# Moving spreads, value casts and one output evacuation between engines and batches in a fused attention and feed-forward kernel

## The chip, the cores and the metric

The kernel runs on 1 core of one Trainium2 chip. The metric is device time in microseconds (us), lower is better. Most executions of this kernel agree within about 1 %. Below, TensorE, VectorE, ScalarE and GpSimd are the engines that the profile calls PE, DVE, ACT and POOL, and SyncE (SP) issues transfers.

## The reference

```python
# attention: 8 batches, 8 heads, 576 positions, head size 64
scores = (q @ k.T) / 8                       # per batch and head
# heads 0-3: the last 32 positions; heads 4-7: every 4th of the last 128
attn = softmax(where(mask, scores, -1e9))
x = (attn @ v), heads side by side           # 4608 tokens x 512
# feed-forward
h = x @ w_in                                 # 512 -> 2048
g = h * sigmoid(beta * h)
out = g @ w_out                              # 2048 -> 512, float32
```

## The kernel before

The tokens go through the feed-forward part in nine tiles of 512. While TensorE does tile t, the steps of the attention of batch t+1 are slipped in between its matmul groups, in an order written down by hand:

```python
SECOND = "K2 Q2 K3 Q3 v0 S20 v1 S21 S22 S23 ... V10 X00 V11 X01 X10 X11".split()   # beside tile 0
THIRD  = "d0 d1 v0 S20 S21 S22 k0 S23 v1 V20 S30 k1 V21 S31 q0 ...".split()        # beside tile 1
# S: scores and exp (from the third batch on, a mask multiplied in on GpSimd)
# V: values times scores, then 1/sum on VectorE;  X: transpose back to xT
# d, k, q: spreads (VectorE copies transposed data into zero-padded tiles)
# v0, v1: casts of the dilated heads' values, v2 / v4, v5: of the plain heads'
```

The third batch's q and k come by a detour: a casting write to a scratch in DRAM (GpSimd's queue), then four transposing loads on SyncE's queue, and behind these the loads of its values:

```python
for kind in "kq": cast_qk(2, kind)        # GpSimd: scratch write
for kind in "kq": load_dil(2, kind)       # SyncE: kdT, qdT
for kind in "kq": load_plain(2, kind)     # SyncE: kpT, qpT
...
at("X20", load_vd, b + 1, SQ)             # SyncE: values, behind the four transposes
```

A step's instructions go into each engine's queue in the order of the list, and every queue is worked off in order. One feed-forward group is 4 matmuls of 128x512; "o" groups (output part) have w_out in place of w_in:

```python
tnh = tanh(beta/2 * hps)                  # ScalarE
g   = (tnh + 1) * hps                     # VectorE, frees the PSUM bank
...
nc.scalar.mul(out=osb, in_=ops, mul=0.5)  # an output group leaves PSUM
```

The softmax here doesn't subtract the row's maximum and nothing guards it: scores larger than these inputs give would overflow.

Of the kernel before, what the change touches and what calls it, by code (L numbers as in the profile page):

```python
# [11 lines left out]
ALU = mybir.AluOpType  # L12
# [5 lines left out]
STEPS = (  # L18
    "S20 S21 S22 k0 S23 k1 V20 S30 q0 V21 S31 q1 V22 S32 q2 V23 S33 q3 V30 X20 S00 V31 S01 X21 V32 "
    "S02 V33 S10 V00 X30 S11 V01 S12 X31 V10 X00 V11 X01 X10 X11"  # L20
).split()
# [4 lines left out]
    "z1 z2"  # L26
).split()
SECOND = (
    "K2 Q2 K3 Q3 v0 S20 v1 S21 S22 S23 K0 K1 S30 V20 S31 Q0 V21 S32 V22 S33 V23 V30 S00 "
    "V31 X20 v2 S01 V32 S02 V33 S10 X21 S11 V00 X30 S12 V01 X31 V10 X00 V11 X01 X10 X11"  # L30
).split()
THIRD = (
    "d0 d1 v0 S20 S21 S22 k0 S23 v1 V20 S30 k1 V21 S31 q0 V22 S32 q1 V23 S33 q2 q3 V30 X20 S00 V31 "
    "S01 X21 V32 S02 V33 v2 S10 V00 X30 S11 V01 S12 X31 V10 X00 V11 X01 X10 X11"
).split()


@with_exitstack
def kernel(
# [10 lines left out]
    nc = tc.nc  # L50
# [43 lines left out]
    def bank(dt=FP32):  # L94
# [32 lines left out]
    k1 = [xT[:, 2 * i:2 * i + 2, 2 * S:2 * S + WIN + S] for i in range(2)]  # L127
    q1 = [qq[i][:].rearrange("p a b c d -> p (a b c d)").rearrange(
        "p (x h t) -> p x h t", x=2, h=2) for i in range(2)]
# [14 lines left out]
    def zeros_kz():  # L144
        for i in range(2):
            nc.gpsimd.memset(kz[i][64:128, :, :, 0], 0.0)
            nc.gpsimd.memset(kz[i][0:64, :, :, 1], 0.0)
# [51 lines left out]
    def build_masks_d():  # L199
        for hf, lo in enumerate(LO):  # L200
            band(mask_d[hf][:].rearrange("p a b n -> p (a b) n"), DQ[hf], -lo, WIN - 1 - lo,
                 1.0, 0.0)
# [26 lines left out]
    def load_w_in(c0, c1):  # L229
        nc.gpsimd.dma_start(  # L230
            out=w_in_bf[:, :, c0:c1], in_=moe_w_in[:, c0:c1].rearrange("(c p) d -> p c d", p=P))

    def load_w_out(g):
        nc.gpsimd.dma_start(
            out=w_out_bf[:, g * 4:(g + 1) * 4, :],
            in_=moe_w_out[g * 4 * P:(g + 1) * 4 * P, :].rearrange("(c p) d -> p c d", p=P))
# [86 lines left out]
    def cast_v(b, n, eng):  # L323
        if n == 2 or n > 3:
            h = slice(0, 4) if n == 2 else slice(2 * n - 8, 2 * n - 6)
            copy_on(eng)(out=vp[b % 2][:, h, :, 0:D], in_=vp_st[b % 2][:, h])
        else:
            f, K = (slice(n, n + 1), DK[n]) if n < 2 else (slice(0, 2), 96)
            copy_on(eng)(  # L329
                out=vd[b % 2][0:K, f].rearrange("p f h T e -> p (f h T) e")[:, :, 0:D],  # L330
                in_=vd_st[0:K, f].rearrange("p f h T d -> p (f h T) d"))
# [147 lines left out]
    def attention_step(b, name):  # L479
        if name[0] == "W":  # L480
            for n in range(int(name[1:])):
                nc.tensor.matmul(warm_ps[:], lhsT=warm_w[:, 0:P], rhs=warm_w[:], start=True, stop=True)
        elif name[0] == "H":
            early[0] = -1
            slot_h(0, int(name[1:]), (2, 3))
        elif name[0] in STEP:
            STEP[name[0]](b, *[int(c) for c in name[1:]])
        else:
            eng = (nc.scalar if name[0] == "v" and (b, name) in ((1, "v2"), (2, "v0"), (2, "v1"), (2, "v2")) else
                   nc.gpsimd if b == 0 and name in ("v1", "v4", "v5") else nc.vector)  # L490
            BRING[name[0]](b, int(name[1:]), eng)

# [37 lines left out]
    def slot_o(t, tb, part):  # L530
        if (t, tb) == (NTT - 1, 3):
            last_o(t, tb, part)
            return
        if part == 0:
            if t > NTT - 3 and tb:
                o_t[t, tb] = psum_at.tile([P, HD], FP32, name="at")
            elif t == 0 and tb == 2:
                o_t[t, tb] = psum_h.tile([P, HD], FP32, name="h_ps")
            else:
                o_t[t, tb] = psum_o.tile([P, HD], FP32, name="o_ps")  # L540
        ops = o_t[t, tb]
        for fb in range(4 * part, 4 * part + 4):
            nc.tensor.matmul(  # L543
                ops[:], lhsT=g_t[t, fb][:, tb * P:(tb + 1) * P], rhs=w_out_bf[:, fb, :],
                start=(fb == 0), stop=(fb == NFB - 1))
        if part == 3:
            osb = osb_pool.tile([P, HD], FP32, name="osb")
            nc.scalar.mul(out=osb[:], in_=ops[:], mul=0.5)  # L548
            later.append([2, lambda: store(t * NTOK + tb * P, osb)])


# [27 lines left out]


    def steps(b):
        return SECOND if b == 1 else THIRD if b == 2 else STEPS

    def extras(b):
        e = {}
        at = lambda name, fn, *a: e.setdefault(steps(b).index(name), []).append(lambda: fn(*a))
        V, A, G = nc.vector, nc.scalar, nc.gpsimd
        SQ = nc.sync
        if b + 1 < B:
            if b > 1:  # L590
                if b == 2:
                    at("S20", gate, raw[2, "q"][0:1, 0:1])
                for kind in "kq":
                    at("S20", cast_qk, b + 1, kind)
                at("X20", load_vd, b + 1, SQ)
                at("X20", load_vp, b + 1, SQ)
            if b == 1:
                at("X20", load_vd, b + 1, SQ)
                at("X20", load_vp, b + 1, SQ)
            if b > 1:  # L600
                for kind in "kq":
                    at("V21", load_dil, b + 1, kind)
                for kind in "kq":
                    at("V30", load_plain, b + 1, kind)
            if b > 1:
                at("S11", spread_dil, b + 1, 0, V)
                at("V01", spread_dil, b + 1, 1, V)
                at("X00", cast_v, b + 1, 3, G)
                at("X01", cast_v, b + 1, 2, G)
        return e  # L610


    SQ, G, A, V = nc.sync, nc.gpsimd, nc.scalar, nc.vector
# [20 lines left out]
    for name in FIRST:  # L634
        if name == "v1":
            attention_step(0, "v1")
            build_neg_p()
            for c0, c1 in ((0, 256), (256, 512), (512, 1024)):
                load_w_in(c0, c1)
            continue  # L640
        if name == "v5":
            for n in "kq":
                load_tok(1, n, 1)
            load_w_in(1024, 2048)
            make_identity(nc, ident_f[:])
        if name == "X10":
            build_beta()
        attention_step(0, name)
# [12 lines left out]
    for kind in "kq":  # L661
        load_plain(2, kind)
    load_w_out(3)
    zeros_kz()
    build_masks_d()
    build_masks_p()

# [1 line left out]
    at_once = [3, 2] + [1] * (NTT - 3) + [4]  # L669
    WORK = {"S": 3, "V": 3, "X": 2, "d": 3, "K": 3, "Q": 3, "k": 0, "q": 0, "v": 1}  # L670
    left = []
    first = lambda n: max(0, (n - 4) // 2) if n < 14 else 3 * n - 37
    for t in range(NTT):
        slots = []
        n = len(left)
        for fb in range(NFB):
            slots.append((slot_h, t, fb, (0, 1)) if (t, fb) in h_t else (slot_h, t, fb))
            while left and n - len(left) < n * (fb + 1) // NFB:
                slots.append(left.pop(0))
        left = [(slot_o, t, tb, part) for tb in range(4) for part in range(4)]  # L680
        if t == 0:

            left = [(slot_o, 0, tb, part) for part in range(4) for tb in range(3)] + left[12:]
            for n, tb in ((10, 0), (13, 1)):
                left.remove((slot_o, 0, tb, 0))
                slots.insert(n, (slot_o, 0, tb, 0))
        now = 4 * at_once[t] - (2 if t == 0 else 0)
        slots += left[:now]
        left = left[now:]
        b = t + 1  # L690
        work = list(enumerate(steps(b))) if b < B else []
        e = extras(b) if b < B else {}
        e0 = list(work)
        room = [(1 if fn is slot_h else 2) if n >= FROM.get(t, 0) else 0
                for n, (fn, *_) in enumerate(slots[:-2])]
        total, whole, done, seen = sum(room), sum(WORK[s[0]] for m, s in work), 0, 0
        for n, (fn, *args) in enumerate(slots):
            fn(*args)
            seen += room[n] if n < len(room) else 0
            while work and (done * total < whole * seen if t else len(e0) - len(work) < first(n)):  # L700
                m, name = work.pop(0)
                done += WORK[name[0]]
                for x in e.get(m, []):
                    x()
                attention_step(b, name)
            tick()
# [32 lines left out]
```

## Time and profile before

| | before |
|---|---|
| time, median of 3 runs | 335.06 us (334.36 to 336.41) |
| profiled execution | span 332.5 us |
| tile 0, tile 1, tile 2, each later full tile | 42.95, 34.44, 31.21, 33.09 us |

A tile is counted here from the weight load of its first matmul group to that of the next tile. In the page's list of busy time, TensorE leads by far (busy us, share of span, instructions):

```profile
PE 315.6 (95%) x2426; PEld 167.0 (50%) x2426; DVE 194.9 (59%) x432; ACT 199.0 (60%) x382; POOL 131.8 (40%) x172
```

The 5 % that TensorE is idle lie in the first 125 us and in the last slice, where the kernel runs out.

### The profile page before, as it was taken

The page shows a single profiled execution, that of the slowest core. Times are in us where ns is not written, and L with a number is a line of the kernel's source. Part 1 is how long each engine was busy: PE and PEld are TensorE (multiplying, and loading weights), DVE is VectorE, ACT ScalarE, POOL GpSimd, SP SyncE. Part 2 cuts the span into 40 slices and gives each one's busy share as a digit, 9 for nine tenths or more (in the row PEclk, how much of TensorE's full clock was granted, in tenths as well). Part 3 has the DMA queues.
Part 4 walks back from the last instruction along what each step waited for, and adds up shares of the span by engine and source line. Part 5 has one row for each costly group of instructions (what it writes and reads, how often), then busy time and mean ns, then how long its engine had stood idle before and what let it go on. Part 6 is the DMA issues. An engine that isn't in the chain of part 4 may idle for free.

```text
span 332.5 us, 6380 instructions
## 1 busy us (share of the span) xinstructions
PE 315.6 (95%) x2426; PEld 167.0 (50%) x2426; DVE 194.9 (59%) x432; ACT 199.0 (60%) x382; POOL 131.8 (40%) x172
## 2 busy tenths in 40 slices
PE   8888989997899899999999999999999999999995
PEld 3653456544455455555555555555555544444444
DVE  4668585479657775777376737673766344344400
ACT  3577566685757666666666666666666545355511
POOL 8883595133385346533653365335533000000000
PEclk9999999999999999999999999999999999999999
DMA  6999999999899795999598958792011210011131
GB/s 113 205 199 196 216 255 172 202 199 197 170 163 157 139 190 111 147 208 146 103 176 170 149 103 175 176 142 63 3 34 32 63 35 33 32 34 32 32 95 65
DMA packets 64927, 42.63 MB, mean 128 GB/s; under 512 B 48896, under 2 KB 58784, under 8 KB 64512
## 3 DMA queue, kind: packets, MB, share of 16 engines
q1 hardware_dynamic: 57264, 25.58, 41.2%
q0 software_dynamic: 7632, 16.64, 27.7%
q8 instruction: 19, 0.31, 0.4%
q14 instruction: 12, 0.10, 0.1%
HBM read 39.32 MB, written 16.52 MB: 168 GB/s over the span
## 4 chain that ended last, share of the span: by engine, by line
PE 80%; DMA 6%; DVE 5%; ACT 3%; POOL 3%; issue 1%; POOLq 0%; ACTq 0%; DVEq 0%
PE h_ps L505 30%; PE o_ps L543 28%; PE at L543 5%; DMA w_out_bf<-in_moe_w_out_dram 4%; PE at L443 4%; PE at L460 3%; DVE g L515 2%; DMA xT<-in_k_dram 2%; PE at L410 2%; PE at L417 2%; PE at L505 2%; ACT tnh L512 1%; PE at L358 1%; PE h_ps L543 1%; DVE qq L294 1%
## 5 line engine op out<-in xcount | busy, mean ns | idle before, releaser
L515 DVE SCALAR_TENSOR_TENSOR g<-tnh,h_ps 128x512 bf16<-128x512 bf16 x130 | 88.8, 684 | 90.0 <-ACT tnh L512 89.4
L505 PE MATMUL h_ps<-xT,w_in_bf 128*128 128x512 bf16 x520 | 131.0, 379 | 2.6 <-DVE g L515 2.1
L512 ACT ACTIVATE tnh<-h_ps,beta_half 128x512 bf16<-128x512 f32 x130 | 89.4, 687 | 57.6 <-PE h_ps L505 53.7
L543 PE MATMUL o_ps<-w_out_bf,g 128*128 128x512 bf16 x464 | 116.9, 379 | 0.7 <-DMA w_out_bf<-in_moe_w_out_dram 0.7
L505 PEld LDWEIGHTS <-w_in_bf 128*128 128x128 bf16 x576 | 51.5, 98 | 52.9 <-issue 3.4
L543 PEld LDWEIGHTS <-g 128*128 128x128 bf16 x560 | 50.2, 97 | 48.7 <-issue 1.0
L425 POOL TENSOR_TENSOR pt<-pt,mask_d 96x384 bf16<-96x384 bf16 (+1 forms) x48 | 36.8, 776 | 50.6 <-ACT pt L423 50.0
L423 ACT ACTIVATE pt<-at 128x384 bf16<-128x384 f32 (+2 forms) x107 | 45.9, 439 | 16.6 <-PE at L410 8.6
L450 DVE TENSOR_TENSOR xs<-at,rcp 48x256 bf16<-48x256 f32 (+2 forms) x91 | 42.1, 463 | 8.9 <-PE at L460 4.8
L425 POOL TENSOR_TENSOR pt<-pt,mask_PP 128x384 bf16<-128x384 bf16 x24 | 22.8, 950 | 37.5 <-ACT pt L423 37.4
L443 PEld LDWEIGHTS <-pt 128*128 128x128 bf16 (+2 forms) x448 | 24.3, 97 | 14.9 <-DVE vd L329 1.2
L548 ACT ACTIVATE osb<-o_ps 128x512 f32<-128x512 f32 x29 | 17.3, 597 | 19.4 <-PE o_ps L543 19.4
L417 PEld LDWEIGHTS <-kdT 128*96 128x96 bf16 (+1 forms) x128 | 14.3, 120 | 10.9 <-issue 1.5
L446 DVE RECIPROCAL rcp<-at 48x4 f32<-48x4 f32 (+2 forms) x91 | 16.0, 176 | 6.0 <-PE at L443 5.3
L543 PE MATMUL at<-w_out_bf,g 128*128 128x512 bf16 x80 | 19.4, 379 | 0.0
L460 PE MATMUL at<-ident_b,xs 96*128 96x96 bf16 (+1 forms) x224 | 17.9, 199 | 1.5 <-DVE xs L450 1.0
L460 PEld LDWEIGHTS <-xs 96*128 96x128 bf16 (+1 forms) x224 | 13.2, 96 | 11.1 <-issue 1.8
L443 PE MATMUL at<-vd,pt 96*128 96x65 bf16 (+1 forms) x244 | 17.3, 193 | 0.7 <-DVE vd L329 0.7
L417 PE MATMUL at<-qzd,kdT 128*80 128x96 bf16 (+1 forms) x122 | 17.1, 226 | 0.8 <-DVE qzd L282 0.8
L425 POOL TENSOR_TENSOR pt<-pt,mask_FP 128x384 bf16<-128x384 bf16 x12 | 10.9, 911 | 16.1 <-ACT pt L423 16.1
L505 PE MATMUL at<-xT,w_in_bf 128*128 128x512 bf16 x56 | 13.8, 379 | 1.4 <-DMA w_in_bf<-in_moe_w_in_dram 1.4
L474 ACT COPY xT<-at 128x384 bf16<-128x384 bf16 (+1 forms) x32 | 12.7, 396 | 2.6 <-PE at L460 2.6
(115 smaller groups left out, 255.1 us busy)
## 6 DMA issues: line engine op xcount, KB each, us to landing
vp_st<-in_v_dram SPq DMA_DIRECT2D x12, 384.0 KB, 8.9
qk<-in_k_dram POOLq DMA_DIRECT2D x6, 576.0 KB, 7.0
qk<-in_q_dram POOLq DMA_DIRECT2D x6, 576.0 KB, 10.4
vd_st<-in_v_dram SPq DMA_DIRECT2D x6, 384.0 KB, 5.3
w_out_bf<-in_moe_w_out_dram POOLq DMA_DIRECT2D x4, 512.0 KB, 17.6
vd_st<-in_v_dram SPq DMA_DIRECT2D x6, 320.0 KB, 6.2
out_dram<-osb SPq DMA_DIRECT2D x7, 256.0 KB, 3.5
out_dram<-osb SPq DMA_DIRECT2D x8, 224.0 KB, 2.4
```

The lines of the kernel that those rows point to most:

```text
L417: nc.tensor.matmul(sc[0:K, a, 0:2 * n], lhsT=kd[b][:, rp, h4, DO[hf]:DO[hf] + K], rhs=qzd[b % 2][:, :, rp, h4, hf * DQ[0]:hf * DQ[0] + n], ...
L423: nc.scalar.activation(out=w, in_=sc[0:K, :, 0:2 * n], func=ACT.Exp, scale=SCALE)
L425: nc.gpsimd.tensor_tensor(out=w, in0=w, in1=mask[0:K], op=ALU.mult)
L443: nc.tensor.matmul(pv[:, a, h2, :], lhsT=pt[x][0:K, c:c + P], rhs=rhs, start=True, stop=True)
L446: nc.vector.reciprocal(out=rcp[0:n, 0:m], in_=pv[0:n, :, :, D])
L450: nc.vector.tensor_tensor(out=xs_t[b, x, jx][:, a0:a0 + m], in0=pv[0:n, :, :, 0:D], in1=rcp[0:n, 0:m].unsqueeze(3).to_broadcast([n, m, 2, ...
L460: nc.tensor.transpose(xp[:, a * n:(a + 1) * n], xs[:, a].rearrange("p h d -> p (h d)"), ident_b[0:n, 0:n])
L505: nc.tensor.matmul(hps, lhsT=w_in_bf[:, kt, fb * P:(fb + 1) * P], rhs=xT[:, kt, t * NTOK:(t + 1) * NTOK], start=(kt == 2), stop=(kt == 1))
L512: nc.scalar.activation(out=tnh[:], in_=hps, func=ACT.Tanh, scale=beta_half[:, fb:fb + 1])
L515: nc.vector.scalar_tensor_tensor(out=g[:], in0=tnh[:], scalar=1.0, in1=hps, op0=ALU.add, op1=ALU.mult)
L543: nc.tensor.matmul(ops[:], lhsT=g_t[t, fb][:, tb * P:(tb + 1) * P], rhs=w_out_bf[:, fb, :], start=(fb == 0), stop=(fb == NFB - 1))
L548: nc.scalar.mul(out=osb[:], in_=ops[:], mul=0.5)
```

## The change

Its intent is to take work off VectorE and ScalarE where they hold up TensorE, in tiles 0 and 1, and to bring forward the weights that arrive late. Its core:

```diff
-SECOND: "K2 Q2 K3 Q3 v0 S20 v1 S21 ..."            -> no v0, v1, v2
+SECOND: "K2 Q2 K3 Q3 S20 S21 ..."
-THIRD:  "d0 d1 v0 S20 S21 S22 k0 S23 v1 V20 S30 k1 V21 S31 q0 V22 S32 q1 V23 S33 q2 q3 V30 ..."
+THIRD:  "S20 S21 S22 q0 S23 V20 S30 q1 V21 S31 q2 V22 S32 q3 V23 S33 V30 ..."
+FOURTH: as the later batches, with q3 ahead of S33, V31 ahead of S00 and X21 ahead of S01
 # third batch's spreads, during the second batch's attention, on VectorE
+                at("V10", spread_dil, b + 1, 0, V)
+                at("V11", spread_dil, b + 1, 1, V)
+                at("X01", spread_k, b + 1, 0, V)
+                at("X10", spread_k, b + 1, 1, V)
 # third batch's dilated value casts: from ScalarE to GpSimd, ahead of its masks
+                if b == 2:
+                    at("S20", cast_v, b, 0, G)
+                    at("S20", cast_v, b, 1, G)
 # second batch's value casts: from VectorE and ScalarE to GpSimd
     load_w_out(3)
+    for n in range(2):
+        cast_v(1, n, G)
     zeros_kz()
+    for n in (4, 5):
+        cast_v(1, n, G)
 # weights: first half of this piece of w_in ahead of the second batch's q and k
+            load_w_in(1024, 1536)
             for n in "kq":
                 load_tok(1, n, 1)
-            load_w_in(1024, 2048)
+            load_w_in(1536, 2048)
 # two output groups of tile 0 one h group later
-            for n, tb in ((10, 0), (13, 1)):
+            for n, tb in ((11, 0), (14, 1)):
 # one evacuation of tile 0
-            nc.scalar.mul(out=osb[:], in_=ops[:], mul=0.5)
+            if t == 0 and tb == 1:
+                nc.vector.tensor_single_scalar(out=osb[:], in_=ops[:], scalar=0.5, op=ALU.mult)
+            else:
+                nc.scalar.mul(out=osb[:], in_=ops[:], mul=0.5)
```

(The pacing of the second batch's steps is also refitted to the shorter list.)

## The prediction

> **What bounds the kernel now.** I read first the page's slices, then the busy time by stage (cut where a token tile of the second part begins), then TensorE in order of time. The slices say where there is anything to win:
>
> ```profile
> PE   8888989997899899999999999999999999999995
> PEclk9999999999999999999999999999999999999999
> ```
>
> TensorE is at full clock throughout, and the digits below 9 lie before about 125 us. Behind that it never waits: the tiles from 130.7 us on take 33.09 us each with 33.07 busy. So the end is set by TensorE, and a microsecond that it stops waiting before 130 us is a microsecond off the end. By stage (the h matmuls of tile 0 begin in full at 24.72, of tile 1 at 64.72, tile 2 at 99.33, tile 3 at 130.70; columns: window, wall, then busy us and instruction counts of PE, PEld, DVE, ACT, POOL, clock, DMA share, GB/s):
>
> ```profile
> 24.72:64.72 40.00, 36.00 (x358) 20.22 (x357) 26.83 (x55) 25.61 (x51) 20.90 (x32) 1.00 1.14 210
> 64.72:99.33 34.61, 30.61 (x240) 15.86 (x238) 23.60 (x50) 23.80 (x46) 15.83 (x18) 1.00 0.99 176
> 99.33:130.70 31.37, 30.05 (x238) 16.12 (x237) 22.13 (x48) 20.57 (x41) 15.74 (x18) 1.00 0.93 152
> 130.70:163.79 33.09, 33.07 (x254) 17.69 (x252) 21.48 (x48) 21.48 (x42) 16.11 (x18) 1.00 0.89 156
> ```
>
> TensorE idles 4.0 us in tile 0, 4.0 in tile 1, 1.3 in tile 2: 9.3 us is all that there is. The timeline of TensorE names the waits (in brackets: idle before, releaser):
>
> ```profile
> 33.22 1.04 PE L505 MATMUL at<-xT,w_in_bf 128*128 128x512 bf16 x4 [1.36 <-DMA w_in_bf<-in_moe_w_in_dram]
> ...
> 36.33 1.02 PE L543 MATMUL o_ps<-w_out_bf,g 128*128 128x512 bf16 x4 [0.70 <-DMA w_out_bf<-in_moe_w_out_dram]
> ...
> 45.75 0.62 PE L358 MATMUL at<-ident_b,xT 64*64 64x64 bf16 x18 [1.15 <-DVE g L515]
> ...
> 69.97 0.50 PE L417 MATMUL at<-qzd,kdT 128*96 128x192 bf16 x4 [0.76 <-DVE qzd L282]
> ...
> 78.57 1.02 PE L505 MATMUL h_ps<-xT,w_in_bf 128*128 128x512 bf16 x4 [1.08 <-DVE g L515]
> ...
> 80.46 1.02 PE L505 MATMUL h_ps<-xT,w_in_bf 128*128 128x512 bf16 x4 [0.74 <-DVE g L515]
> ...
> 113.28 0.34 PE L410 MATMUL at<-qq,kz 128*128 128x96 bf16 x4 [1.30 <-DVE qq L294]
> ```
>
> Each is a target of the change: the first two are weights that arrive late, the rest are VectorE late with a spread, or with the product g because spreads and casts stand in its queue.
>
> **What the Trainium skill says.** "GPSIMD Engine Reference", section Engine selection, has two-input work about twice as slow on GpSimd as on VectorE, and one-input work "roughly line-rate". The trace agrees on the casts: GpSimd's 96x2048 cast took 1.89 us, so I take 0.95 to 1.0 us for half of it; ScalarE's 96x1024 took 1.03. "SBUF — State Buffer", section SBUF: two separate sides, calls the port pair that VectorE and GpSimd share an exclusive lock. The trace fits: VectorE's value casts at 43 to 47 us, while GpSimd cleared kz, took 1.87 and 1.35 us, against 0.62 at best for this cast. "Trainium Kernel Development and Optimization", section Key Constraints, says that transfers issued from SyncE and GpSimd run on the same 16 DMA engines and interleave. The trace agrees: the third batch's value loads, issued in the busiest stretch, took 7.7 and 8.5 us, where the medians of the like are 5.3 and 6.2.
>
> **The change part by part.**
>
> Tile 0 (second batch's attention). The w_in load is halved and its first half goes ahead of a q/k load, so the 1.36 us wait should go. The first w_out block still lands at 22.03 + 14.25 = 36.3 us, but the order of instructions shows that one h group (4 x 0.216 = 0.86 us) and one transposing step (12 transposes, 0.40) now run before TensorE needs it. Work that used to follow 36.33 is done by then: 1.26 us won, not 2.06, with a smaller wait left. The value casts leave VectorE (1.87 + 1.35 us beside g), and the transposes behind 45.75 no longer wait for a g; I count 0.9 of that 1.15. At the end two output groups instead of one lie behind the last normalizations, and cover the two dilated spreads (0.45 us each) put between them. Their data is just there: that transpose is issued at 54.5 and lands 5.1 us later, at 59.6. Sum: tile 1 starts some 2.3 us early, near 62.4.
>
> On GpSimd the moved casts wait for values that land at 43.2 and 44.5 us (issued at 25.7 and 27.6, 17.5 and 16.9 us under way), then kz (6 us), two half casts (0.82 each) and the masks (8.2) follow to about 61.5. Before, masks ended at 54.6 and GpSimd waited 7.6 us until 62.2 for the gate. This fits into that wait and costs nothing.
>
> Tile 1 (third batch). VectorE loses two dilated spreads (0.92 us in all) and two k spreads (0.61 + 1.03), ScalarE two value casts (1.03 each). But **the third batch's value casts now stand in GpSimd's queue ahead of the masks of its attention**, and their data is late:
>
> ```profile
> 60.19 1.03 SPq L320 DMA_DIRECT2D vd_st<-in_v_dram  x2
> ...
> vd_st<-in_v_dram SPq DMA_DIRECT2D x1, 384.0 KB, 7.7
> vd_st<-in_v_dram SPq DMA_DIRECT2D x1, 320.0 KB, 8.5
> ```
>
> These loads queue on SyncE behind four transposes, which wait for the second q/k scratch write (37.93 + 16.6 = 54.5 us). TensorE being earlier moves none of this. So values land at 60.2 + 7.7 = 67.9 and 60.7 + 8.5 = 69.2. Before, ScalarE took the first at 68.97, and the second not until 73.86; GpSimd's masks did not depend on them. Now: second cast from 69.2 to 70.2, mask of the first score group to 71.1, of the second to 72.1 (0.91 each). The first value product V20 reads 32 columns past its own group, so its last weight load waits for the second mask too (the order shows both waits): it ends near 72.15. TensorE would be there after 6 groups (5.2 us), four score groups (0.5) and small waits, at 62.4 + 6 = 68.4. **A new wait of about 3.7 us**; tile 0's gain and more is spent in it.
>
> What it buys: V20 now stands two h groups earlier in TensorE's order, so its time is not to be compared with 73.07 directly. From V20 to the last part of tile 0's outputs the kernel before took 73.07 to 89.09, 16.02 us, with VectorE busy for 13.91: VectorE's stretch. The same stretch has now 11 h groups instead of 9. TensorE: 13 groups of 0.864 = 11.2, 7 score groups 1.1, 7 value groups of 0.14 = 1.0, two transposes 0.37, in all 13.7. VectorE: 11 g of 0.68 = 7.5, normalizations 3.7, three q spreads 1.5, in all 12.7; the k spreads (1.64) and one q spread are gone. So TensorE leads, plus 0.4 of small waits: 14.1. That output part starts at 72.15 + 14.1 = 86.3, 2.8 us before 89.09. The 10.24 us from there to tile 2 stay.
>
> Tile 2 (fourth batch). Its last q spread moves ahead of one g in VectorE's order (0.67 us) and a value group and an h group stand before the score group that waits for it. Of the 1.30 I count 1.0. One vector osb (some 0.6 us) for one on ScalarE is hidden. Tiles 3 to 7 have the same order as before.
>
> **Sum:** 335.06 - 2.8 - 1.0 = 331.3 us.
>
> **Rivals.**
> (a) The waits simply go. Of the waits named above, 1.26 + 0.9 in tile 0, 0.76 + 1.08 + 0.74 and two of 0.3 in tile 1, 1.0 in tile 2 make 6.3, so 328.8. For it: no engine is full in tile 1. Against it: the values' landing time above, which no part of the change moves. If they landed 2 us earlier, as in later batches, this is the result.
> (b) GpSimd becomes the bound further on. For it: casts, masks and the shared lock. Against it: it was busy 15.8 of 34.6 us in tile 1, and after V20 its masks need 0.9 us to about 2 us of TensorE. If slow casts (1.4 us each, as one of 80x1024 took 1.47) and one more stall come, 332.5 to 333.
> (c) VectorE stalls in front of the moved spreads, as qdT lands at 59.6. Tile 1 then starts up to 1 us later, but V20 has 3.7 us of slack against that: no difference.
>
> **Range and chances.** The landing of the values carries most of the error: a microsecond there is a microsecond. The tile 1 stretch is good for 0.7 either way, tile 2 for 0.4. I say 331.3, 329.3 to 333.4. Over 2% faster means below 328.4: only rival (a) with nothing lost, 0.07. Slower by 2% would need over 6.7 us of new waits beyond the one I know: 0.01.
>
> **What would show it.** The w_in wait at 33 us gone and the w_out wait shorter; tile 1 starting at 62 to 63; then TensorE idle for 3 to 4 us at 68 to 72, released by a GpSimd mask, with GpSimd waiting for the vd_st transfer until 68 to 69; no idle over 0.8 us from VectorE at 75 to 90; tile 2 starting near 96.5, tile 3 near 127; from there 33.1 us a tile. I am wrong if V20 runs by 69 or 70, if tile 1 starts later than 65, or if the idle of VectorE's making stays.

## The result

The changed kernel took 331.23 us in the median of 4 runs, 330.29 to 335.36, against 334.93 us before (4 runs). A ratio here is the mean time of one kernel's runs over that of the other's of the same rounds, so not quite the ratio of the medians: 0.9874, 95 % interval 0.9837 to 0.9911. Executions over 1.5% slower than the fastest of the same kernel are left out of the means. The same, unchanged file ran twice more among the experiments: 1.0003 (0.9939 to 1.0066) and 0.9946 (0.9898 to 0.9993). All three are within 2 % of before.

The first profile fell in a slow execution (335.36 us), the second (after_again) had a stretch of half clock. The third (after_third, span 329.5 us) ran at full clock from start to end, as the profile of before did, and started its tile 0 at the same moment (21.65 and 21.72 us). These two are compared. By stage, columns as in the prediction:

```profile
24.65:63.46 38.81, 35.21 (x351) 20.18 (x356) 25.75 (x57) 23.92 (x49) 22.75 (x33) 1.00 1.20 206
63.46:97.22 33.76, 30.29 (x233) 16.17 (x237) 22.59 (x48) 21.82 (x42) 18.82 (x23) 1.00 1.09 194
97.22:127.37 30.15, 29.82 (x234) 15.99 (x237) 22.29 (x48) 20.55 (x41) 16.12 (x19) 1.00 0.91 155
```

Some matmul records are missing from this trace (PE's instruction counts are lower than PEld's), so its busy time is low by about a per cent, and the walls are what to read. Between weight loads, tile 0 went from 42.95 to 41.77 us, tile 1 from 34.44 to 33.77, tile 2 from 31.21 to 30.15: 1.2 + 0.7 + 1.1 = 3.0 us, the whole difference of the spans (332.5 to 329.5). From there both kernels take 33.1 us a tile.

TensorE's waits in the timeline of after_third, to set beside those in the prediction:

```profile
36.02 1.02 PE L549 MATMUL o_ps<-w_out_bf,g 128*128 128x512 bf16 x4 [0.73 <-DMA w_out_bf<-in_moe_w_out_dram]
...
61.26 0.30 PE L466 MATMUL at<-ident_b,xs 96*128 96x96 bf16 x3 [0.32 <-DVE xs L456]
62.63 0.30 PE L466 MATMUL at<-ident_b,xs 96*128 96x96 bf16 x3 [1.07 <-DVE xs L456]
...
70.25 0.20 PE L449 MATMUL at<-vd,pt 96*128 96x65 bf16 x1 [0.60 <-POOL pt L431]
77.54 1.02 PE L511 MATMUL h_ps<-xT,w_in_bf 128*128 128x512 bf16 x4 [0.84 <-DVE g L521]
79.16 1.02 PE L511 MATMUL h_ps<-xT,w_in_bf 128*128 128x512 bf16 x4 [0.48 <-DVE g L521]
...
89.01 0.34 PE L449 MATMUL at<-vp,pt 128*128 128x65 bf16 x6 [0.89 <-ACT vp L332]
```

The w_in wait at 33 us, the one of 1.15 at 45, the spread's at 70 and the one of 1.30 at 113 are gone. New are the wait of V20's last matmul for a mask on GpSimd, which the prediction foresaw at 3.7 us and which is 0.60, and 1.39 us in front of the last transposes of tile 0, where before there were 0.52. The wait for ScalarE's cast of the third batch's plain values (vp) grew from 0.24 to 0.89. The chain of waits tells where those come from (start, duration, what):

```profile
54.34 5.45 DMA qdT<-qk
...
59.82 0.63 DVE qzd L288
...
60.65 0.55 DVE xs L456
...
61.23 0.46 DVE qzd L288
...
62.02 0.56 DVE xs L456
...
62.63 0.30 PE at L466 x3
```

The dilated q transpose of the third batch lands, the first moved spread (qzd) can run, and only behind it comes the normalization (xs) of the second batch that TensorE waits for; then the second spread, and the last normalization. Work for the next batch, waiting for its own data, stands in VectorE's queue in front of work that TensorE needs now.

### The profile page after: what moved, and what is told of

Same layout as the page of the kernel before. It is cut to its first block, busy times and chain, and to the rows that moved or that the text cites. A ratio compares the mean times of both kernels' runs of the same rounds, so it can differ in the third digit from the quotient of the medians.

```text
span 333.7 us, 6338 instructions
## 1 busy us (share of the span) xinstructions
PE 315.5 (95%) x2382; PEld 168.8 (51%) x2426; DVE 192.8 (58%) x431; ACT 195.4 (59%) x378; POOL 137.0 (41%) x179
## 4 chain that ended last, share of the span: by engine, by line
PE 71%; DMA 15%; POOL 4%; DVE 3%; SPq 2%; issue 2%; ACT 2%; POOLq 0%; ACTq 0%; DVEq 0%
PE h_ps L511 30%; PE o_ps L549 26%; PE at L549 5%; DMA qk<-in_q_dram 5%; DMA xT<-in_k_dram 4%; DMA vp_st<-in_v_dram 3%; PE at L449 3%; DMA vd_st<-in_v_dram 2%; PE at L466 2%; PE at L416 2%; PE at L423 2%; DVE g L521 1%; POOL xT L261 1%; SPq L279 1%; PE at L568 1%
## 5 line engine op out<-in xcount | busy, mean ns | idle before, releaser
L549 PE MATMUL o_ps<-w_out_bf,g 128*128 128x512 bf16 x443 | 113.6, 379 | 1.2
L466 PEld LDWEIGHTS <-xs 96*128 96x128 bf16 (+1 forms) x224 | 13.7, 97 | 14.4 <-DVE xs L456 4.1
L335 POOL CAST vd<-vd_st 96x2048 bf16<-96x2048 f32 (+2 forms) x10 | 14.6, 1460 | 10.6 <-DMA vd_st<-in_v_dram 7.3
L480 ACT COPY xT<-at 128x384 bf16<-128x384 bf16 (+1 forms) x32 | 12.7, 396 | 4.9 <-PE at L466 4.9
```

The costliest lines, as they stand in the source:

```text
L466: nc.tensor.transpose(xp[:, a * n:(a + 1) * n], xs[:, a].rearrange("p h d -> p (h d)"), ident_b[0:n, 0:n])
L549: nc.tensor.matmul(ops[:], lhsT=g_t[t, fb][:, tb * P:(tb + 1) * P], rhs=w_out_bf[:, fb, :], start=(fb == 0), stop=(fb == NFB - 1))
```

## The experiments

Twelve runs were made, two of them of the unchanged file. The theories: the third batch's arrivals (transposes, values) bound the stretch from 60 to 72 us, so a wait taken away in front of them comes back at them; or the load of the engines does, with the arrivals hidden. All outputs were correct.

First, what disturbs every comparison. In 8 of the 14 profiles TensorE ran at half clock in one or more windows of 3.4 us before 25 us, when the kernel is just starting, whatever the kernel. Tile 0 then begins at 22.8 to 26.2 us instead of 21.1 to 21.7. So I give the start of tile 0 with each profile, and read the lengths of the stages rather than only the times, whose intervals reach 0.3 to 0.7 % to either side:

| run | ratio to before (95 %) | tile 0 start | tile 0 | tile 1 | tile 2 | span |
|---|---|---|---|---|---|---|
| before | | 21.72 | 42.95 | 34.44 | 31.21 | 332.5 |
| after (slow) | 0.9874 (0.9837 to 0.9911) | 23.82 | 43.15 | 34.34 | 30.16 | 333.7 |
| after_again | 1.0003 (0.9939 to 1.0066) | 21.45 | 42.71 | 34.76 | 30.16 | 331.3 |
| after_third | 0.9946 (0.9898 to 0.9993) | 21.65 | 41.77 | 33.77 | 30.15 | 329.5 |
| casts_on_act | 0.9984 (0.9941 to 1.0027) | 26.16 | 40.04 | 33.62 | 30.16 | 332.2 |
| spreads_late | 0.9962 (0.9897 to 1.0027) | 21.10 | 40.08 | 36.52 | 30.16 | 330.0 |
| early_qk | 1.0000 (0.9946 to 1.0055) | 22.84 | 41.76 | 34.01 | 30.16 | 331.0 |
| keep_warm | 0.9978 (0.9942 to 1.0014) | 23.45 | 41.26 | 33.08 | 30.16 | 330.1 |
| spreads_behind | 0.9917 (0.9877 to 0.9958) | 24.91 | 39.56 | 34.15 | 30.16 | 331.0 |
| behind_v20_late | 0.9904 (0.9865 to 0.9943) | 21.59 | 39.97 | 36.40 | 30.16 | 330.3 |
| only_fourth | 0.9947 (0.9915 to 0.9979) | 24.18 | 40.27 | 34.43 | 30.16 | 331.2 |
| split_casts | 0.9936 (0.9891 to 0.9981) | 21.61 | 39.85 | 35.15 | 30.14 | 328.9 |
| split_casts_late | 0.9927 (0.9879 to 0.9974) | 26.08 | 39.42 | 34.75 | 30.15 | 332.6 |
| only_weights | 1.0019 (0.9962 to 1.0077) | 24.62 | 39.94 | 34.43 | 31.20 | 332.3 |

The runs came in three groups, each with its own runs of the kernel before: after_again, casts_on_act, spreads_late and early_qk on one chip; keep_warm, spreads_behind, behind_v20_late and only_fourth on another; after_third, split_casts, split_casts_late and only_weights on that second chip again. There is one profile of each run, so the lengths of the stages are single executions.

### The changed kernel again

No edit. 

> The changed kernel once more, for a profile in the fast state (the first one fell in a slow execution, 335.36 us). Theory 1 (the third batch's arrivals bound the stretch from 60 to 72 us): 331.2 us, ratio 0.987; TensorE idles for 2 to 4 us in all between 58 and 73 us, in front of a last transpose of tile 0 (VectorE waits for the dilated q transpose, rival (c) of the prediction) or of the first value product V20, or both. Theory 2 (engine load bounds it and the arrivals are hidden): under 1 us of such idle, and the time left over is spread over waits for VectorE after 75 us.

> The changed kernel a third time, beside its rivals on one chip, in five rounds. The first set of rounds gave a ratio of 0.987, the second 1.000 with a wide interval. If the half clock at 64 to 68 us comes in most executions: about 333, ratio 0.994, and the profile shows it. If it was chance: 331, ratio 0.988.

TensorE idled 2.5 us before 64 us in after_again (1.47 and 1.07 at the last transposes of tile 0, VectorE having waited 2.0 for qdT) and 1.4 in after_third. So theory 1 has the place, and it is mostly the spreads, not V20. The 1.07 us is the same in all three profiles of the changed kernel and so belongs to the order of VectorE's work; only the wait ahead of it (1.70 us in the first profile, 1.47, 0.32) moves with the landing of qdT. In after_again TensorE's clock was halved right afterwards, from 64.5 to 67.9 us, as it was in the first, slow profile (64.9 to 68.3); in after_third it was not. The time did not settle at either value of the expectation.

### One spread late, or none early

```diff
 # spreads_late
-                at("V10", spread_dil, b + 1, 0, V)   (and the other three)
-THIRD: "S20 S21 S22 q0 S23 V20 S30 q1 ..."
+THIRD: "d0 d1 S20 S21 S22 k0 S23 V20 S30 k1 V21 S31 q0 ..."
```

> The changed kernel with the four spreads of the third batch (two dilated, two k) back in the third batch's own attention, q spreads as before; value casts stay on GpSimd. Theory 1: the wait in front of the end of tile 0 goes, the wait of V20 for the values and masks grows by about as much, and VectorE has 2.6 us more in tile 1: 1 to 2.5 us slower than the changed kernel, 332 to 333.5. If the early spreads' wait for their transpose is lost time that nothing else takes up: equal to the changed kernel or faster, 331 or below.

Tile 0 became 40.08 us long, against 41.77 and 42.71 in the changed kernel with a like start, and tile 1 began at 61.18 us: early spreads cost 1.7 to 2.6 us there. But tile 1 got 2.7 us longer than in after_third, and in front of its first score groups stands

```profile
67.92 0.50 PE L423 MATMUL at<-qzd,kdT 128*96 128x192 bf16 x4 [2.05 <-DVE qzd L288]
```

So the two placements differ by 0.5 us at the start of tile 3 (127.85 against 127.33). The wait came back at another place, but not as theory 1 has it. qdT was issued at 53.96 us and landed after 6.3, at 60.3. VectorE sat idle from 60.93 to 63.17 us and came to the first spread only behind three g's:

```profile
65.56 0.45 DVE L288 COPY qzd<-qdT 64x1152 bf16<-64x1152 bf16 x1
```

The second spread began at 66.64 and took 1.14 us. So the 2.05 us are the spreads' place in VectorE's queue, which neither theory names: the data had been there for 5 us. The expected loss of 1 to 2.5 us in the time was not seen (0.9962 against 1.0003 on that chip, the intervals overlap).

### The casts back on ScalarE

```diff
 # casts_on_act
-                    at("S20", cast_v, b, 0, G)       (and 1)
-THIRD: "S20 S21 S22 q0 S23 V20 ..."
+THIRD: "v0 S20 S21 S22 q0 S23 v1 V20 ..."           # v0, v1 on ScalarE
```

> The changed kernel with the third batch's two dilated value casts back on ScalarE, in the places of before. Theory 1: the masks no longer stand behind the values, but V20 needs the first cast itself, and the spreads still wait for their transpose: the same within 1 us of the changed kernel, ratio to before 0.985 to 0.991. If GpSimd's queue is what costs (the 3.7 us of the prediction), it gains 1.5 us or more, ratio below 0.983.

No faster: 0.9984. Its profile started late (26.16 us), so that nothing waited for qdT in VectorE and tile 1 began at 66.2. V20 still waited 0.61 us for a mask, whose exp now stood behind the cast (69.85 to 70.88 us) in ScalarE's queue. So the times show no gain of the 1.5 us that GpSimd's queue was expected to cost; the profile cannot test it, since the first values had landed at 68.8 us, before TensorE needed them.

### The scratch writes earlier

```diff
 # early_qk
+    for kind in "kq": cast_qk(2, kind)
     load_w_out(2)
     load_vp_1(1, G)
-    for kind in "kq": cast_qk(2, kind)
```

> The changed kernel with the third batch's q/k scratch writes issued ahead of the third w_out block and the second batch's plain values. The transposes and the value loads behind them then come some 4 us sooner; w_out and the values some 3 us later, still before use. Theory 1: the waits at 60 to 72 us shrink by 2 to 3 us and the time falls to 328 to 329.5, ratio about 0.98. Theory 2: no change, 331. If the delayed w_out block is used before it lands, a new wait in tile 0 gives part back.

A miss: 1.0000. The two dilated transposes were issued 5.6 to 6.0 us sooner than in after_again (45.91 and 48.89 us), but took 14.2 and 12.1 us to land instead of about 6, which I put down to the w_out block and the values that now share the engines with them; the last transpose was issued at 59.98 us, 1.3 later than in after_again. That the bytes before 60 us bound the arrival, whatever their order, fits this but is not shown: the edit also made GpSimd wait 6.2 us for the second batch's plain values, until 56.58. Its mask building ended at 66.6 us instead of 60.1 (after_third), and the third batch's first cast began at 67.85, though its values had landed at 66.6.

### Keeping TensorE busy through the wait

```diff
 # keep_warm: nine matmuls of zeros that nobody reads
+                at("X10", keep_warm, 5)
+                at("X11", keep_warm, 4)
```

> The changed kernel with nine matmuls of zeros put into the two waits at the end of tile 0 (five before the step X10, four before X11, 1.9 us in all); nothing reads them. Both profiles of the changed kernel so far show TensorE at half clock for 3.4 us right after these waits (64.5 to 67.9 us, 64.9 to 68.3 us). Theory A (TensorE's idleness there makes the clock drop, and the drop takes some 1.7 us): no half clock between 60 and 72 us, the waits look shorter by what the zeros fill, and tile 2 starts 1 to 1.7 us sooner than in the changed kernel of the same chip. Theory B (the drop is chance, or costs nothing because V20 waits for GpSimd's mask anyway): tile 2 starts no sooner, time as the changed kernel or up to 0.5 us more.

By stage, the window before the drop and the drop in after_again (PEclk is the third last column):

```profile
61.10:64.50 3.40, 1.42 (x11) 0.78 (x12) 3.10 (x9) 0.80 (x2) 1.20 (x3) 0.99 0.98 238
64.50:67.90 3.40, 3.40 (x10) 1.22 (x8) 1.16 (x2) 1.28 (x2) 1.86 (x2) 0.50 1.46 236
```

and the same stretches in keep_warm:

```profile
61.10:64.50 3.40, 3.40 (x22) 1.68 (x21) 3.03 (x7) 1.40 (x5) 0.49 (x2) 1.00 0.64 154
64.50:67.90 3.40, 3.40 (x18) 1.66 (x18) 1.09 (x3) 2.25 (x5) 2.54 (x4) 1.00 1.27 206
```

With the gap filled, the clock stayed; at half clock, 10 matmuls of the span's second window were done, without, 18. Tile 1 took 33.08 us from 64.71, against 34.76 from 64.17 in after_again: 1.7 us, which is half of 3.4. TensorE's waits inside tile 1 are equal in the two, 0.84, 0.48, 0.24 and 0.89 us (0.47 for 0.48 in keep_warm). This shows what a drop takes from tile 1. It does not show that the drop comes in most executions, and the kernel as a whole was not faster (0.9978; the changed kernel on that chip, in other rounds, 0.9946): the zeros are no remedy. "TensorE: Matmul & The Clock Gate" in the Trainium skill, section What's actually happening, describes the gate: it halves the clock after an idle window of some 3.4 us, and the window is free-running. The trace agrees with the length (3.4 us each time) and with the halving, and the free running fits that like gaps did and did not lead to a drop: spreads_late, with TensorE busy for 1.37 us of 64.5 to 67.9, kept its clock.

### The spreads behind the normalizations, and V20 later

```diff
 # spreads_behind
-                at("V10", spread_dil, b + 1, 0, V)
-                at("V11", spread_dil, b + 1, 1, V)
-                at("X01", spread_k, b + 1, 0, V)
-                at("X10", spread_k, b + 1, 1, V)
+                at("X01", spread_dil, b + 1, 0, V)
+                at("X01", spread_dil, b + 1, 1, V)
+                at("X10", spread_k, b + 1, 0, V)
+                at("X11", spread_k, b + 1, 1, V)
 # behind_v20_late, on top
-THIRD: "S20 S21 S22 q0 S23 V20 S30 q1 V21 S31 ..."
+THIRD: "S20 S21 S22 q0 S23 S30 q1 S31 V20 q2 V21 ..."
```

> The changed kernel with the two dilated spreads moved from before V10 and V11 to before X01, behind both normalizations, the k spreads one step further. VectorE then waits for the dilated q transpose with nothing of tile 0 behind it. Theory A: the two waits at the end of tile 0 (2.5 us) go, so does the half clock, tile 1 starts near 61.5, and V20 waits 2 to 3.5 us for GpSimd's masks, as the prediction had it; in all 1 to 2 us faster than the changed kernel. Theory B (arrivals alone bound it): the wait only moves to V20, no faster than the changed kernel.

> As spreads_behind, and V20 two places later in the third batch's order, behind the score groups S30 and S31, so that TensorE has more to do until the values and masks are there. If V20's wait for the masks is what then bounds: 1 to 2 us faster than spreads_behind, 329 to 330. If VectorE is what bounds tile 1 after 72 us: no faster.

Tile 0 fell to 39.56 and 39.97 us: no wait at its end. In behind_v20_late, which started at full clock, tile 1 began at 61.57 us, and V20 then waited although two h groups later in the order:

```profile
71.41 0.27 PE L449 MATMUL at<-vd,pt 96*128 96x65 bf16 x3 [1.73 <-POOL pt L431]
72.28 0.24 PE L449 MATMUL at<-vd,pt 96*128 96x65 bf16 x1 [0.61 <-POOL pt L431]
```

followed by a half clock from 71.8 to 75.2 us. This is the wait of the prediction, in the place it named: it shows once tile 0 no longer waits. spreads_behind started late (24.91), and its V20 waited 0.87 us. By the times, 0.9917 and 0.9904, V20's later place is not the 1 to 2 us faster that was expected of it. The changed kernel did not run in these rounds, so the gain over it that theory A expects is not settled.

### The casts split between two engines

```diff
 # split_casts, on top of spreads_behind: first cast on ScalarE right before V20
-                    at("S20", cast_v, b, 0, G)
-                    at("S20", cast_v, b, 1, G)
+                    at("S30", cast_v, b, 1, G)
-THIRD: "S20 S21 S22 q0 S23 V20 ..."
+THIRD: "S20 S21 S22 q0 S23 v0 V20 ..."
 # split_casts_late: "... S23 S30 v0 q1 V20 S31 V21 ..."
```

> As spreads_behind, with the first of the third batch's dilated value casts on ScalarE right before V20 and the second on GpSimd behind the first four masks. If GpSimd's masks standing behind the value casts are what holds V20: V20's wait falls to 1 us or less, tile 3 starts near 127 us in a run without half clock, 1 us faster than spreads_behind. If the landing of the first values itself (67 to 68 us, plus 1.03 us for the cast) is what holds it: no more than 0.5 us faster.

> As split_casts, with V20 one place later, behind S30. If V20's wait is still above 0.5 us in split_casts: 0.3 to 0.9 us faster than it. If not: equal.

Now V20's masks do not stand behind a cast, and the wait names the cast on ScalarE (timelines of split_casts and, second, of split_casts_late):

```profile
69.22 0.28 PE L449 MATMUL at<-vd,pt 96*128 96x65 bf16 x4 [1.71 <-ACT vd L335]
...
74.29 0.28 PE L449 MATMUL at<-vd,pt 96*128 96x65 bf16 x4 [1.71 <-ACT vd L335]
```

The values, issued at 61.04 us, took 5.6 to land, until 66.6; ScalarE came to its cast at 68.14, behind the tanh of the h group just before V20, and gave 1.03 us to it. In split_casts_late they landed at 67.0 us and lay there until 73.21, and the wait is the same 1.71. So this wait is the cast's place in ScalarE's queue, not the landing; a cast placed one tanh earlier was not tried. In split_casts V20 ran 1.0 us sooner than in after_third, whose profile starts like this one, and the span is 328.9 against 329.5. In five rounds on one chip the difference does not show (0.9936 and 0.9927 against 0.9946). Of all versions none is clearly faster than the changed kernel; the lowest ratios, 0.9904 and 0.9917, come from other rounds, and their intervals overlap its.

### Single parts on the kernel before

```diff
 # only_fourth: before, and
-        return SECOND if b == 1 else THIRD if b == 2 else STEPS
+        return SECOND if b == 1 else THIRD if b == 2 else FOURTH if b == 3 else STEPS
 # only_weights: before, and load_w_in(1024, 1536) ahead of load_tok, the two o groups at 11 and 14
```

> The kernel before with the fourth batch's new order alone (last q spread one place earlier, V31 before S00). The prediction counts 1.0 us for it: tile 2 lasts 30.1 to 30.3 us instead of 31.2, ratio 0.997. If the wait only moves: tile 2 at 31.2, ratio 1.000.

> The kernel before with the w_in load halved and reordered and the two output groups of tile 0 one h group later, nothing else. The prediction counts 1.26 us at this place. If the third batch's arrivals bound what follows: tile 1 starts 1 us or more sooner in the profile (for the same start of tile 0), and the first score group of the third batch waits longer for its spread or VectorE for its transpose, so the time falls by 0.3 to 1.0 us, ratio 0.997 to 0.999. If nothing holds it afterwards: 1.3 us, ratio 0.996.

The new order of the fourth batch alone takes tile 2 from 31.21 to 30.16 us, as in every version that has it. only_weights is inconclusive: 1.0019, and its profile started at 24.62 us, where no weight is late. That itself is telling. only_fourth has tile 0 of the kernel before and the same w_in order as it; with TensorE starting 2.5 us later (24.18 instead of 21.72), its tile 1 began at 64.46 instead of 64.68. A late start cost nothing, since other waits went with it: of the 2.06 us for the weights 0.46 were left, at 37.03 us in front of the first group that reads w_out, and the 1.15 at 45 us was gone. By these profiles, what the weights' new order gains, it gains only in executions whose start was at full clock. By the table, tile 0 without the waits for weights and spreads takes 39.4 to 40.3 us. Not tried alone: the second batch's casts, and the evacuation on VectorE.

## Why the prediction was right, and where its steps were not

The time, the range and the class held: 331.3 predicted, 331.23 measured in the first set. That the two agree to 0.1 us is luck: the same file had medians of 333.39 and 332.59 in its other sets. In the matched full-clock profiles the gain is 3.0 us, where the steps give 3.8; over the three sets, ratios of 0.987, 1.000 and 0.995. By its own signs it is not clean either: it called itself wrong if V20 ran by 69 or 70 or if idle of VectorE's making stayed, and three of V20's four matmuls began at 69.38, the last at 70.25, and VectorE's waits stayed. Step by step, against after_third:

- **Weights in tile 0: right.** w_in's wait is gone, w_out's is 0.73 and its group starts at 36.02 with the same work more behind it. The 1.15 at 45 us went altogether; I had counted 0.9. It also went in only_fourth, which keeps the casts on VectorE but started later (the first took 0.94 us there, not 1.87), so the move of the casts is not the only thing that removes it.
- **End of tile 0: wrong.** "At the end two output groups instead of one lie behind the last normalizations, and cover the two dilated spreads". One of them stands ahead of X10 and the other behind X11, with nothing between X10 and X11, so each spread lengthens the path by its own 0.46 to 0.63 us, and more where qdT is late. Tile 1 started at 63.42, not near 62.4. Rival (c) named this, and said that it would cost nothing since V20 had to wait anyway. That holds for the net (0.5 us between late and early spreads) but overlooks the half clock: in 2 of 3 profiles of the changed kernel it followed this gap.
- **V20's wait: right in kind, too long.** Predicted 3.7 us up to 72.15; measured 0.60 in front of its last matmul, at 70.25. The mis-sized term is the landing of the values. They were issued at 59.99 and 61.44 us and landed after 5.9 and 5.9 us instead of 7.7 and 8.5. GpSimd's timeline:

```profile
66.01 1.03 POOL L335 CAST vd<-vd_st 96x1024 bf16<-96x1024 f32 x1 [1.18 <-DMA vd_st<-in_v_dram]
67.41 1.04 POOL L335 CAST vd<-vd_st 80x1024 bf16<-80x1024 f32 x1 [0.37 <-PE h_ps L511]
68.41 3.01 POOL L431 TENSOR_TENSOR pt<-pt,mask_d 96x384 bf16<-96x384 bf16 x4
```

The casts and masks are as long as estimated; the rest of the missing wait was already spent at the end of tile 0, since TensorE came a microsecond later.

- **The stretch after V20: wrong, in two ways.** I took 89.09 us for the start of the output part that ends it; in the trace that part starts at 87.94, and what lies at 89.09 is the next one. So the stretch took 14.87 us before, not 16.02, and 11.4 us lie behind it, not 10.24. And TensorE does not lead in it yet. By window, kernel before and after_third:

```profile
73.07:87.94 14.87, 12.38 (x98) 6.43 (x97) 13.25 (x28) 9.93 (x19) 5.43 (x8) 1.00 0.89 173
70.45:85.94 15.49, 13.77 (x103) 7.33 (x103) 11.67 (x27) 9.54 (x18) 5.86 (x8) 1.00 1.16 215
```

VectorE's load fell, by more than computed (from 13.25 to 11.67 us, where I had 12.7), but its order still makes TensorE wait 0.84, 0.48 and 0.27 us for a g. The two h groups more (1.73 us) cost 0.62 us net: the change won 1.1 us here, not the 3.6 that 16.02 + 1.73 - 14.1 claims. The predicted and the measured start of the output part, 86.3 and 85.94, agree because the values came 1.7 us early and the stretch took 1.4 us longer. Two errors cancelled; the number was better than its derivation.

- **Tile 2: right.** 1.0 predicted, 1.06 measured, 1.05 with this part alone.
- **Rival (a), all waits simply going, fell** as expected: 328.8 us was not reached. Its reason, the arrivals, is only part of it. Of the waits left in tile 1, the 0.60 at V20 is theirs; 1.59 are VectorE's with a g, and 0.89 are ScalarE's cast of the plain values.

The lesson of the spread between sets is not in the prediction at all: start-up windows at half clock, different in each execution, shift TensorE against the transfers by up to 5 us, so each execution meets a different set of these waits. That they make the ratio differ by over a per cent between sets is a reading of the profiles; the timed runs have no traces, so it is not shown.

## What to carry to other kernels

Work for the next stage that waits for its own transfer must not stand in an in-order queue ahead of what the current stage needs: behind it, the same wait is free until the next stage asks. A wait that comes back at another place need not be a transfer's: compare when the data landed with when the engine came to it. In spreads_late, split_casts and split_casts_late the data had lain there for 5.3, 1.5 and 6.2 us, and the place in a queue was the cause. And check each term of a sum against its own row of the trace: a total that fits does not prove the terms.

## What the Trainium skill lacked or had wrong

- "TensorE: Matmul & The Clock Gate" says that the clock is halved after an idle window and does not say how little work counts as idle. Here drops followed windows in which TensorE was busy for 1.21 (after), 1.42 (after_again) and 1.55 (behind_v20_late) of 3.40 us; the array need not be idle for a whole window. Busy time alone does not decide it: in windows laid out in steps of 3.41 us from a run's own clock changes, 1.69 us (split_casts_late, from 72.3 us) and 1.90 (early_qk, from 60.7) brought no drop, but 2.16 (after, from 13.7) and 2.60 (keep_warm, from 11.3), in part transposes, did.
- "SBUF — State Buffer", section SBUF: two separate sides, has the exclusive lock between VectorE and GpSimd. The runs fit it, and one case shows what it cost: a q spread that takes 0.46 us took 1.74 us at 68.77 us in after_third, where GpSimd went from a cast to four masks.
- "GPSIMD Engine Reference", section Engine selection, calls one-input work "roughly line-rate" where it sets GpSimd beside VectorE. The 96x1024 cast took 1.03 us on GpSimd and 1.03 on ScalarE, but 0.62 on VectorE (at 11.98 us in after_third): moved off VectorE it grew by two thirds.
- No page says how far a load's time to landing may be off when the 16 DMA engines are full: the first of the two value loads, at about the same place in every version, took 4.7 to 7.8 us.
